# Squares of token tiles 8 to 11 moved from TensorE and VectorE to ScalarE, with a new order on every engine

## The chip, the cores and the metric

The kernel runs on one core of a Trainium2 chip. The metric is the device time of one execution in microseconds. A lower time is better.

## The reference

One transformer layer on 2048 tokens of width 640 in bfloat16: a LayerNorm, a linear attention with 32 heads of 20 numbers each (softmax feature maps of both signs), a projection with a residual, a second LayerNorm, and a gated bilinear feed-forward of width 1536 with a residual.

```python
def _A_ref(x, wqkv, w_phi, wo):
    qkv = (x @ wqkv).reshape(B, S, 3, H, Dh)            # -> q, k, v per head
    pq = jnp.einsum("bhsd,hdf->bhsf", q, w_phi)
    pk = jnp.einsum("bhsd,hdf->bhsf", k, w_phi)
    phi_q = concat([softmax(pq), softmax(-pq)], axis=-1)
    phi_k = concat([softmax(pk), softmax(-pk)], axis=-1)
    kv = jnp.einsum("bhsf,bhsd->bhfd", phi_k, v)
    z  = jnp.einsum("bhsf->bhf", phi_k)
    num = jnp.einsum("bhqf,bhfd->bhqd", phi_q, kv)
    den = jnp.einsum("bhqf,bhf->bhq", phi_q, z)[..., None] + 1e-6
    return (num / den).reshape(B, S, D) @ wo

h  = x + _A_ref(layernorm(x), wqkv, w_phi, wo)
h2 = h + ((g := layernorm(h) @ w_gate) * (layernorm(h) @ w_up)) @ w_down
```

The first `layernorm(x)` is what the change touches: for each token it needs the mean and the mean of the squares over 640 numbers.

## The kernel before, in words

The 2048 tokens are 16 tiles of 128. Each operation is recorded with `g.op` under the name of a unit (`U`). `ORDER` gives for each engine a written list of unit names; an engine carries out its operations in exactly that order, each one once what it needs is there. `Prog.place` walks through the five lists with the costs given to each operation (`t`, `lat`, `size`) and decides from them which of the rotating buffers an operation gets; it moves nothing. `Prog.finish` puts the semaphore waits between the engines. SP's list is a queue of DMA issues: loads, and transposes done by the DMA engines.

The names of the units: `wk` and `x0` to `x4` build the folded key weights, `t0` to `t4`, `wm`, `wq0` to `wq4` and `y0` to `y4` the folded query weights, `wv` and `c0` to `c4` centre the value weights. `lT4` to `lT15` are the transposed loads of a token tile (`xT`), `lx0` to `lx3` the plain loads of four token tiles each (`x_all`, so `lx2` holds tiles 8 to 11), `lwq`, `lwo`, `lg`, `lu`, `ld` the loads of the query, output, gate, up and down weights. `s0`, `s2`, `s4`, `s8`, `s12` are the statistics of token tiles 0-1, 2-3, 4-7, 8-11, 12-15. `k`, `v`, `q` with a tile number are the projections of keys, values and queries; `K` and `Q` normalise keys and queries. `A0` to `A14` accumulate keys times values, `Aout` brings that to SBUF, `n` is the numerator with its division, `h` the output projection with residual and second LayerNorm, `wo0` to `wo4` sum Wo's rows on ScalarE, `f` are feed-forward steps, `d` and `D` the down projection, and `G`, `H`, `S`, `T` sums for matrix products that need fewer multiplications.

All matrix products land in four PSUM buffers of two banks each (`p_ps`). A group of matmuls takes a buffer when one is free and gives it back when its last reader is through. For keys and queries (`softexp`) that is VectorE's maximum (L925), a product on VectorE (L928) and two exponentials on ScalarE (L933); for values one evacuation by ScalarE (L956).

The statistics are in `stats`. In the form for all tiles but 12 to 15, TensorE multiplies each of the five 128x128 blocks of a tile by itself and by a column of constants, 129 columns in all; the diagonal of the sum holds the sums of squares, which VectorE reads out with one multiply-and-sum pass over 128x128 per tile (L702), and the last column is the sum. For tiles in a group named in `ST_ACT`, TensorE only multiplies by the column of constants (one column), and ScalarE squares the tile in its natural layout (`x_all`, loaded by `lx`) and sums it on the way (`act_sum`, L650). GpSimd then makes the reciprocal standard deviation (`rs`, `nrs`) from both, and the exponentials of keys and queries and the evacuation of values need it.

Of the kernel before, what the change touches and what calls it, by code (L numbers as in the profile page):

```python
# [11 lines left out]
P = 128  # L12
S = 2048
D = 640
NT = S // P
NC = D // P
# [41 lines left out]
ST_ACT = (12,)  # L58
# [39 lines left out]
    "DVE":  # L98
# [16 lines left out]
    "ACT":  # L115
# [318 lines left out]
def _build(ctx, nc, A_x, A_wqkv, A_w_phi, A_wo, B_w_gate, B_w_up, B_w_down, out):  # L434
    g = Prog(nc, ctx)
# [8 lines left out]
    x_all = sb([P, NT, D], BF16, "x_all")  # L444
# [1055 lines left out]
```

## Time and profile before

| what | value |
|---|---|
| median of 3 runs | 267.67 us (267.41 to 268.5) |
| profiled execution | 267.55 us, span 265.8 us |
| granted clock | 0.999 |
| TensorE busy | 260.4 us (98% of the span) |
| TensorE weight loads busy | 200.0 us (75%) |
| VectorE busy | 222.7 us (84%) |
| ScalarE busy | 177.2 us (67%) |
| GpSimd busy | 190.1 us (72%) |
| data moved by DMA | 28.65 MB, mean 108 GB/s |

The span runs from the first to the last instruction of the profiled execution; the time also holds what lies around it. A matmul's end is modelled and matmuls overlap, so two matmul groups are compared by their starts, and a wait of TensorE is looked for on its weight loads (PEld), which come ahead of the matmuls. A row of the timeline has the start and the duration in us, the engine, the line, the operation, what it writes and reads, and in brackets the idle time ahead of it with what ended it. A row of the waits has who waited for whom, the total in us, how often, and the longest.

### The profile page before, as it was taken

To read this page: it belongs to the slowest core of one execution; us is meant where nothing else is said; L and a number is where in the kernel's file an instruction comes from. 1 tells how busy PE (TensorE), PEld (TensorE's weight loads), DVE (VectorE), ACT (ScalarE), POOL (GpSimd) and SP (SyncE) were. 2 spreads that over 40 slices of the span, in tenths; PEclk is the share of its full clock that TensorE was granted. 3 is DMA by queue.
4 is the path that set the end of the run, shared out by engine and by line. 5 is a ranking of instruction groups with operands and counts; after the bars stand their busy time and mean duration, and the time that the engine had idled before them with its cause. 6 is when DMAs were issued, how large, how long until landed. Compare 5 with 4: busy or idle time off the path is not lost.

```text
span 265.8 us, 6243 instructions
## 1 busy us (share of the span) xinstructions
PE 260.4 (98%) x2418; PEld 200.0 (75%) x2433; DVE 222.7 (84%) x417; ACT 177.2 (67%) x387; POOL 190.1 (72%) x243
## 2 busy tenths in 40 slices
PE   8999999999999999999999999999999999999995
PEld 8877777776877787777767887777777777777773
DVE  1999999999999876998999778988778788675683
ACT  2567999999857998769553695764857555645220
POOL 5446989999932889999974789359866575648652
PEclk9999999999999999999999999999999999999999
DMA  7997999903155789666856515300410401001012
GB/s 188 302 138 175 165 233 401 382 32 75 39 82 100 89 247 210 130 106 133 131 115 128 47 25 79 99 4 0 56 45 19 83 0 52 1 2 51 14 65 71
DMA packets 67390, 28.65 MB, mean 108 GB/s; under 512 B 57632, under 2 KB 66080, under 8 KB 67360
## 3 DMA queue, kind: packets, MB, share of 16 engines
q1 hardware_dynamic: 66432, 27.90, 48.7%
q10 hardware_dynamic: 928, 0.35, 0.5%
q8 instruction: 19, 0.31, 0.5%
q14 instruction: 11, 0.09, 0.1%
HBM read 11.82 MB, written 2.62 MB: 54 GB/s over the span
## 4 chain that ended last, share of the span: by engine, by line
PE 85%; DVE 5%; DMA 3%; ACT 3%; issue 1%; POOL 1%; SPq 0%; ACTq 0%
PE ps L657 60%; PE ps L1210 24%; DMA phiqT<-eq 3%; ACT eq L933 1%; DVE ob L1075 1%; PE ps L746 1%; DVE x_all L1093 1%; DVE ps L925 1%; DVE Sq L987 1%; ACT phiqT L1335 0%; POOL eq L999 0%; DVE rden L1073 0%; DVE phiqT L806 0%; ACT junk L650 0%; ACT eq L1220 0%
## 5 line engine op out<-in xcount | busy, mean ns | idle before, releaser
L657 PE MATMUL ps<-Wp,xT 128*128 128x320 bf16 (+1 forms) x606 | 89.1, 299 | 0.0
L657 PEld LDWEIGHTS ps<-Wp,xT 128*128 128x128 bf16 x606 | 58.0, 98 | 22.5 <-ACT phik L933 0.3
L1240 POOL TENSOR_TENSOR phik<-phik,gate 128x512 bf16<-128x512 bf16 x34 | 40.1, 1184 | 25.9 <-DVE phik L1237 25.5
L1220 ACT ACTIVATE eq<-ps 128x256 f32<-128x256 f32 x110 | 37.4, 386 | 23.0 <-PE ps L1210 18.6
L1210 PE MATMUL ps<-phik,Wgu 128*128 128x256 bf16 (+1 forms) x214 | 46.6, 299 | 0.2
L950 POOL TENSOR_TENSOR phik<-phik,Rk 128x1280 bf16<-128x1280 bf16 x16 | 37.4, 2357 | 5.8 <-DVE Rk L949 4.8
L657 PE MATMUL ps<-phik,Wgu 128*128 128x256 bf16 (+1 forms) x259 | 33.2, 280 | 0.1
L657 PEld LDWEIGHTS ps<-phik,Wgu 128*128 128x128 bf16 x260 | 25.0, 98 | 5.5
L1337 POOL TENSOR_TENSOR phiqT<-phiqT,x_all 128x320 f32<-128x320 f32 x26 | 21.7, 844 | 9.7 <-ACT phiqT L1335 9.6
L925 DVE TENSOR_REDUCE ps<-ps 128x1 f32<-128x640 f32 (+1 forms) x32 | 26.1, 818 | 2.8 <-PE ps L657 2.8
L1210 PEld LDWEIGHTS ps<-phik,Wgu 128*128 128x128 bf16 x228 | 21.9, 98 | 5.7 <-ACT eq L1220 0.2
L657 PE MATMUL ps<-vaug,phik 128*128 128x63 bf16 (+1 forms) x308 | 25.9, 238 | 0.0
L987 DVE TENSOR_REDUCE Sq<-eq 128x66 f32<-128x1320 bf16 x16 | 24.2, 1513 | 1.4 <-ACT eq L933 1.4
L1237 DVE TENSOR_TENSOR phik<-ps,eq 128x512 bf16<-128x512 f32 x28 | 19.1, 687 | 6.3 <-PE ps L1210 6.2
L1335 ACT ACTIVATE phiqT<-ps 128x320 f32<-128x320 f32 x26 | 11.4, 437 | 19.3 <-PE ps L657 19.2
L947 DVE TENSOR_REDUCE Ssum<-phik 128x64 f32<-128x1280 bf16 x16 | 23.3, 1460 | 0.0
L1235 DVE TENSOR_TENSOR gate<-ps,eq 128x512 bf16<-128x512 f32 x27 | 18.5, 685 | 5.2 <-PE ps L1210 2.9
L657 PEld LDWEIGHTS ps<-vaug,phik 128*128 128x128 bf16 x308 | 18.1, 97 | 5.3
L999 POOL TENSOR_TENSOR eq<-eq,rq 128x660 bf16<-128x660 bf16 x16 | 20.9, 1305 | 0.8
L933 ACT ACTIVATE eq<-ps,nb,rs 128x300 bf16<-128x300 f32 (+2 forms) x26 | 17.2, 689 | 6.1 <-DVE nb L928 4.5
L1342 DVE TENSOR_TENSOR outb<-ps,phiqT 128x320 bf16<-128x320 f32 x28 | 13.4, 487 | 6.9 <-PE ps L657 5.5
L1139 ACT ACTIVATE gate<-ps 128x256 bf16<-128x256 f32 (+1 forms) x26 | 10.4, 406 | 10.3 <-PE ps L657 9.6
(168 smaller groups left out, 526.2 us busy)
## 6 DMA issues: line engine op xcount, KB each, us to landing
x_all<-in_A_x_dram SPq DMA_DIRECT2D x4, 640.0 KB, 10.7
out_dram<-outb SPq DMA_DIRECT2D x14, 160.0 KB, 1.9
Wgu<-in_B_w_gate_dram SPq DMA_DIRECT2D x1, 1920.0 KB, 10.6
Wgu<-in_B_w_up_dram SPq DMA_DIRECT2D x1, 1920.0 KB, 16.3
vaug<-in_B_w_down_dram SPq DMA_DIRECT2D x1, 1920.0 KB, 8.5
Wp<-in_A_wqkv_dram SPq DMA_DIRECT2D x1, 800.0 KB, 5.0
phiqT<-in_A_wqkv_dram SPq DMA_DIRECT2D x1, 800.0 KB, 6.4
Wo<-in_A_wo_dram SPq DMA_DIRECT2D x1, 800.0 KB, 6.0
```

Of the source, the lines that this page charges most:

```text
L657: ins = e.matmul(o_, lhsT=l_, rhs=r_, start=s_, stop=p_, skip_group_check=True)
L925: g.op("DVE", lambda e: e.tensor_reduce(out=mx(), in_=src(), axis=AX.XY if len(src().shape) == 3 else AX.X, op=ALU.max, apply_absolute_val ...
L933: g.op("ACT", lambda e, s=s, sc=sc, to=to, of=of: e.activation(out=to(s), in_=of(), func=ACT.Exp, bias=nb[:, i:i + 1], scale=sc[:, t:t + 1 ...
L947: g.op("DVE", lambda e: e.tensor_reduce(out=Ssum[:, vs.i, :], in_=x, axis=AX.X, op=ALU.add), rd=R_phik[t], wr=vs.R, use=[vs], t=1.39, lat=1.5)
L950: g.op("POOL", lambda e: e.tensor_tensor(out=x, in0=x, in1=Rk[:, vr.i, :].unsqueeze(2).to_broadcast([P, 2 * H, DH]), op=ALU.mult), rd=vr.R ...
L987: g.op("DVE", lambda e: e.tensor_reduce(out=Sq[:, vs.i, :].rearrange("p (w g) -> p w g", w=NQ), in_=feat(0, NQ).rearrange("p w (g f) -> p ...
L999: return e.tensor_tensor(out=x, in0=x, in1=rq[:, vr.i, :].rearrange("p (w h) -> p w h", h=HW).unsqueeze(3).to_broadcast([P, NQ, HW, DH]), ...
L1210: ins = e.matmul(o_, lhsT=l_[0](c), rhs=m_, start=fr, stop=False, skip_group_check=True)
L1220: g.op("ACT", lambda e: e.activation(out=half(s[i], 256 * h, 256 * (h + 1)), in_=PS[v.i][:, bk, 256:512], func=ACT.Copy), rd=[v.R[bk]], wr ...
L1237: g.op("DVE", lambda e: e.tensor_tensor(out=hhT[:, hb_, ft, :], in0=PS[v.i][:, 1, :], in1=half(s[1]), op=ALU.add), rd=[v.R[1]] + s[1].R, w ...
L1240: g.op(eng, lambda e: e.tensor_tensor(out=hhT[:, hb_, ft, :], in0=hhT[:, hb_, ft, :], in1=gate[:, vg.i, :], op=ALU.mult), rd=R_out + vg.R, ...
L1337: g.op("POOL", lambda e: e.tensor_tensor(out=slot(x), in0=slot(x), in1=x_all[:, t, c], op=ALU.add), rd=x.R + [R_h[t]], wr=x.R, use=[x], t= ...
```

## The change

`ST_ACT` gets the group of tiles 8 to 11: their squares are summed by ScalarE on the natural tokens, and TensorE's 20 matmuls for them have one column in place of 129. VectorE's four read-outs of these tiles go. Several of the costs that `place` uses are set anew. The lists of all engines are written anew; ScalarE's list still begins with its first three entries (`in in in`). Shown are the heads of four lists and the changed lines of SP's.

```diff
@@ -55,7 +55,7 @@
...
-ST_ACT = (12,)
+ST_ACT = (8, 12)
...
@@ -73,77 +73,77 @@
     "PE":
-        "warm wk wk wk wk wk wk wk wk wk s0 wk x1 s0 x1 x3 wv wv x2 x0 x0 s2 x4 s2 k0 k0 k0 k0 k0 k3 k1 wm k2 v2 v3 s4 s4 s4 s4 "
-        "v5 k7 v7 k4 k6 v4 k5 y3 v0 y1 s8 s8 s8 s8 y4 k10 y2 y0 v1 s12 s12 k11 q0 s12 s12 k8 k9 v11 q1 v9 v6 k12 k13 v14 v10 v13 "
-        "k14 k15 q2 v8 v15 q5 q3 A0 A0 A2 A4 A6 A8 A2 A4 v12 A6 A8 A10 A10 A12 A14 A12 A14 n0 n1 n0 n1 q7 n0 q4 n1 h0 h1 n2 q6 h1 "
...
+        "warm wk wk wk wk wk wk wk wk wk wk x1 s0 s0 x1 x2 x3 wv wv x0 x0 x4 s2 s2 k0 k0 k0 k0 k0 k1 k3 wm v3 v2 k2 s4 s4 s4 s4 "
+        "k7 v7 k4 v5 k6 y3 v4 k5 y1 v0 s8 s8 s8 s8 k10 y4 y0 v1 y2 k11 s12 s12 s12 s12 q0 k9 k8 v11 q1 v9 k12 v6 k14 k13 v14 v13 "
+        "v10 k15 q2 v8 v15 v12 A0 A2 q3 A0 A4 A6 A8 q5 A2 A10 A4 A6 A8 A12 A10 A14 A12 A14 n0 n1 n0 n1 q7 n0 q4 n1 h0 h1 n2 q6 h1 "
...
     "DVE":
-        "wk in in wk in wk wk wk s0 s0 x1 x3 s0 c2 c1 c0 s2 s2 c4 s2 k0 k0 c3 k3 k3 k1 k1 K0 k2 wq2 wq4 K0 K1 k2 s4 s4 s4 s4 s4 "
-        "K3 K1 k7 wq0 K3 k7 K2 k4 k4 k6 K2 k6 K7 k5 y3 k5 K7 y1 K4 s8 s8 s8 s8 s8 K4 k10 K5 k10 K6 k11 K6 k11 q0 K5 q0 s12 K10 k8 "
-        "k9 k8 K11 K10 K11 q1 k9 K8 q1 Q0 k12 K8 k13 k12 K9 k13 Q0 Q1 K9 K12 k14 Q1 k14 k15 K12 K13 k15 q2 K13 K14 q2 K14 K15 q3 "
...
+        "wk in in in wk wk wk wk s0 s0 s0 x1 x3 c3 c2 s2 c4 s2 s2 k0 k0 c1 c0 k1 k1 k3 wq2 K0 k3 wq4 K0 K1 k2 k2 s4 s4 K1 s4 s4 "
+        "s4 k7 K3 wq0 k7 k4 K3 k4 K2 k6 y3 k6 K2 K7 y1 K7 k5 k5 s8 K4 K4 k10 K5 k10 K6 k11 K6 s12 K5 k11 q0 q0 K10 k9 k8 k8 K11 "
+        "q1 K10 k9 K11 K8 q1 k12 Q0 k12 K9 K8 k13 k14 k13 Q0 K9 k14 K12 Q1 K12 Q1 k15 K13 k15 K13 K14 q2 K14 q2 K15 q3 K15 q3 Q2 "
...
     "ACT":
-        "in in in wk wk wk x2 x0 x4 k0 k0 k3 wm k1 k1 v2 v3 k3 k2 wq1 k2 v5 wq3 k7 v7 k7 k4 k4 v4 k6 k6 k5 v0 k5 s12 y4 y2 s12 y0 "
-        "v1 k10 k10 s12 k11 k11 q0 q0 s12 v11 k8 k8 v9 k9 k9 v6 q1 q1 wo0 v14 k12 k12 v10 k13 wo1 k13 v13 k14 k14 wo2 v8 k15 k15 "
-        "v15 q2 wo4 q2 wo1 q3 q3 v12 wo3 q5 wo3 q5 wo2 wo0 n0 wo4 n1 q7 q7 q4 q4 q4 q4 h0 h1 f0.4.0 h0 f0.4.0 f0.10.0 f0.10.0 "
-        "f0.0.0 q6 f0.0.0 q6 q6 q6 h2 f0.1.0 h3 f0.1.0 q8 f0.11.0 f0.11.0 q8 q8 q8 f0.8.0 f0.8.0 f0.7.0 f0.7.0 h1 f0.5.0 f0.5.0 "
...
+        "in in in wk wk wk x2 x0 x4 k0 k0 wm k1 v3 k1 v2 k3 k3 s8 k2 k2 wq3 s8 wq1 v7 k7 v5 k7 k4 k4 s8 v4 k6 k6 s8 v0 k5 k5 y4 "
+        "y0 s12 v1 y2 k10 s12 k10 s12 k11 k11 q0 q0 s12 v11 k8 k8 v9 k9 k9 q1 v6 q1 k12 k12 wo1 v14 wo0 v13 k13 k13 v10 k14 wo1 "
+        "k14 wo2 v8 k15 k15 v15 v12 wo3 wo2 q2 q2 q3 q3 wo4 wo3 wo4 q5 q5 wo0 n0 n1 q7 q7 q4 q4 q4 q4 h0 h1 f0.10.0 f0.10.0 "
+        "f0.4.0 f0.4.0 h0 f0.0.0 f0.0.0 q6 q6 q6 h2 q6 f0.1.0 f0.1.0 h3 f0.11.0 q8 f0.11.0 f0.7.0 q8 q8 f0.8.0 q8 f0.8.0 f0.7.0 "
...
     "POOL":
-        "in in in in in in in in in in in in pad in in wk s0 s0 s0 in in s0 s2 s0 s2 s2 s0 s2 s2 s2 K0 s4 s4 s4 s4 s4 s4 K3 K1 K2 "
-        "K7 s8 s8 s8 s0 s8 s8 in s8 K4 K6 K5 s12 in s12 s12 s12 s12 K11 pad s12 K10 K8 Q0 Q0 K9 Q1 Q1 K12 K13 K14 K15 Q2 Q2 Q3 Q3 "
-        "Q5 s4 s2 Q5 Q7 Q7 f0.4.0 f0.10.0 s8 Q4 Q4 f0.0.0 h2 f0.1.0 h2 f0.11.0 Q6 h3 Q6 f0.8.0 h3 f0.7.0 f0.5.0 s12 Q8 f0.6.0 Q8 "
-        "T0 h0 f0.2.0 f0.3.0 T0 h1 h0 f0.9.0 Q10 Q10 T2 Q9 T2 h1 h7 Q14 h5 Q14 h7 h7 Q9 h5 h5 T0 T1 Q11 h4 T1 Q11 h6 h4 Q12 h6 "
...
+        "in in in in in in in in in in in pad in in in wk s0 s0 in s0 s0 s0 in s2 in in s2 s0 s2 s2 s2 s2 K0 s4 s4 s4 s4 s4 s4 K1 "
+        "K3 K2 K7 s8 s8 s8 s8 s8 s8 s0 K4 K5 s2 K6 pad s12 s12 s8 s12 s12 K10 s12 s12 K11 K8 Q0 K9 Q0 Q1 K12 K13 Q1 K14 K15 Q2 Q2 "
+        "Q3 Q3 Q5 Q5 Q7 Q7 f0.4.0 s4 f0.10.0 Q4 Q4 h2 h2 f0.0.0 f0.1.0 Q6 f0.11.0 s12 Q6 f0.8.0 h3 f0.7.0 h3 f0.5.0 Q8 f0.6.0 Q8 "
+        "f0.2.0 T0 T0 f0.9.0 Q10 h1 f0.3.0 T2 Q10 h0 h1 h0 T2 Q14 h7 Q14 h7 h5 h7 h5 Q9 Q9 h5 T1 T0 Q11 Q11 T1 h6 h6 h4 h6 h4 "
...
     "SP":
-        "in in in in in in in lwq t4 lT7 lT4 t2 lT5 lT6 t3 t1 t0 lx3 lT10 lT15 lT9 lT11 lT8 lT13 lT14 lT12 lx0 lwo lg lu lx2 lx1 "
-        "Q0 Q1 Q0 Q1 Q2 Q2 Q3 Q3 Q5 Q5 n2 n3 Q7 Q7 Q4 ld Q4 Q6 n7 n5 Q6 Q8 Q8 h3 n4 h2 Q10 Q10 n6 Q14 Q14 Q9 n8 Q9 h5 h7 Q11 Q11 "
-        "n10 h4 h6 n9 Q12 Q12 n11 Q15 n14 Q13 Q13 Q15 n12 h8 n15 h11 n13 h9 h10 d0 d1 D0.1 h14 D0.1 h12 h13 h15 D1.0 D1.0 D1.1 "
+        "in in in in in in in lwq t2 lT4 lT5 t4 lT6 lT7 lx2 t3 t0 t1 lT15 lT8 lwo lT9 lT11 lT10 lT13 lx3 lT14 lT12 lg lx0 lu Q0 "
+        "Q0 lx1 Q1 Q1 Q2 Q2 Q3 Q3 Q5 n2 Q5 n3 Q7 Q7 ld Q4 n7 Q6 Q4 Q6 n5 h3 Q8 Q8 h2 n4 Q10 Q10 n6 Q14 Q14 Q9 h5 Q9 h7 n8 Q11 Q11 "
+        "n10 h4 h6 n9 Q12 Q12 n11 Q15 n14 Q13 Q15 Q13 n12 d1 d0 n15 h8 n13 h11 h10 h9 h14 D0.1 h15 D0.1 D1.0 D1.0 h13 h12 D1.1 "
...
@@ -546,9 +546,9 @@
-        return g.op(eng, lambda e: e.dma_start(out_, in_), wr=wr, dma=("w", 8), t=0.5, lat=0.4 if at else 1.9, size=mb / 0.38, at=at)
-
-    def transpose(out_, in_, rd, wr, use=(), t=1.27, size=1.07, lat=0.5, at=0.0):
+        return g.op(eng, lambda e: e.dma_start(out_, in_), wr=wr, dma=("w", 8), t=0.5, lat=0.4 if at else 0.6, size=mb / 0.38, at=at)
+
+    def transpose(out_, in_, rd, wr, use=(), t=1.27, size=0.45, lat=0.3, at=0.0):
@@ -585,10 +585,10 @@
-        transpose(lambda: xT[:, t, :, 0:P], lambda: A_x[0, P * t:P * (t + 1), :], [], [R_xT[t]], t=1.5, size=0.75, lat=1.25 if at else 2.75, at=at)
+        transpose(lambda: xT[:, t, :, 0:P], lambda: A_x[0, P * t:P * (t + 1), :], [], [R_xT[t]], t=1.5 if at else 1.4, size=0.75 if at else 0.62, lat=1.25 if at else 2.1, at=at)
-        load(x_all[:, 4 * b:4 * b + 4, :], A_x[0, 4 * P * b:4 * P * (b + 1), :].rearrange("(t p) n -> p t n", p=P), [R_x[b]], 1.2)
+        load(x_all[:, 4 * b:4 * b + 4, :], A_x[0, 4 * P * b:4 * P * (b + 1), :].rearrange("(t p) n -> p t n", p=P), [R_x[b]], 0.9)
@@ -684,7 +684,7 @@
-            g.op("PE", f, rd=[R_xT[t], R_one, R_xone], wr=[v.R[j // 2]], use=[v], t=0.125 if act else 0.282, lat=0.275 if act else 0.43)
+            g.op("PE", f, rd=[R_xT[t], R_one, R_xone], wr=[v.R[j // 2]], use=[v], t=0.19 if act else 0.282, lat=0.34 if act else 0.43)
@@ -816,7 +816,7 @@
-        g.op("PE", lambda e: mms(e, mean_mms(PS[v.i][:, 0, :], range(NC), 0)), rd=R_Wnat + [R_one], wr=v.R, use=[v], t=0.64, lat=0.79)
+        g.op("PE", lambda e: mms(e, mean_mms(PS[v.i][:, 0, :], range(NC), 0)), rd=R_Wnat + [R_one], wr=v.R, use=[v], t=0.73, lat=0.88)
@@ -1001,7 +1001,7 @@
-                      b.R + [R_pad], [R_phiqT[bb][k][tt]], [b], t=0.254 * (w1 - w0), size=0.214 * (w1 - w0)))
+                      b.R + [R_pad], [R_phiqT[bb][k][tt]], [b], t=1.3, size=0.5, lat=0.35))
@@ -1369,7 +1369,7 @@
-        transpose(lambda: WT[:, 0, a, :], lambda: A_wqkv[:, P * a:P * (a + 1)], [], [R_WT[0][a]], t=1.5, size=0.75, lat=2.75)
+        transpose(lambda: WT[:, 0, a, :], lambda: A_wqkv[:, P * a:P * (a + 1)], [], [R_WT[0][a]], t=1.4, size=0.62, lat=2.1)
@@ -1383,7 +1383,7 @@
-    load(Wo[:, :, 0:D], A_wo.rearrange("(c p) n -> p c n", p=P), R_Wo, 1.5)
+    load(Wo[:, :, 0:D], A_wo.rearrange("(c p) n -> p c n", p=P), R_Wo, 0.95)

```

98 rows, old and new, of the table ORDER are left out of this document.

## The prediction

> **What bounds the kernel now.** I read the head of the page, then busy time by stage, then what each engine waited for, then single rows of the timeline.
>
> ```profile
> span 265.8 us, 6243 instructions
> PE 260.4 (98%) x2418; PEld 200.0 (75%) x2433; DVE 222.7 (84%) x417; ACT 177.2 (67%) x387; POOL 190.1 (72%) x243
> PE 85%; DVE 5%; DMA 3%; ACT 3%; issue 1%; POOL 1%; SPq 0%; ACTq 0%
> ```
>
> TensorE is on 85% of the chain that ended last and is busy 98% of the span. The average hides the stage that the change touches. Busy time by stage (stretch, its length, then PE, PEld, DVE, ACT, POOL, the granted clock, the DMA share and GB/s):
>
> ```profile
> 20.00:70.00 50.00, 49.94 (x490) 37.23 (x488) 49.57 (x94) 46.95 (x72) 45.58 (x41) 1.00 0.71 199
> 70.00:80.00 10.00, 9.71 (x167) 7.81 (x164) 9.26 (x23) 5.88 (x13) 5.58 (x7) 1.00 0.40 60
> ```
>
> From 20 to 70 us four engines run at 91% or more: TensorE 49.94, VectorE 49.57, ScalarE 46.95, GpSimd 45.58 of 50. ScalarE has 3.05 us left, VectorE 0.43. What TensorE lost to waits is seen on its weight loads. From 4.7 to 80 us, and then from 80 us on (total, times, longest):
>
> ```profile
> PEld ps L657 <- DVE sm L698: 0.6, 2, 0.4
> PEld ps L657 <- DVE Phi L1040: 0.4, 1, 0.4
> PEld ps L657 <- ACT phik L933: 0.3, 1, 0.3
> PEld ps L657 <- DMA phiqT<-in_A_wqkv_dram: 0.3, 1, 0.3
> PEld ps L657 <- DVE sxx L702: 0.2, 1, 0.2
> ```
>
> ```profile
> PEld ps L657 <- ACT eq L933: 0.9, 2, 0.5
> PEld ps L1210 <- ACT eq L1220: 0.8, 4, 0.2
> PEld ps L657 <- issue: 0.2, 1, 0.2
> PEld ps L1210 <- issue: 0.2, 1, 0.2
> ```
>
> That is 1.8 + 2.1 = 3.9 us in all. So no order of the same work can win more than 3.9 us, while a bad order can lose without such a limit. Shorter TensorE work shortens the kernel, but only if the other three full engines keep up.
>
> **The change part by part.**
>
> *TensorE.* For tiles 8 to 11, 20 matmuls with 129 columns become 20 with one column. The two kinds, each with the row that starts next:
>
> ```profile
> 34.13 1.30 PE L657 MATMUL ps<-xT 128*128 128x129 bf16 x20
> 35.26 0.48 PE L657 MATMUL ps<-Phi,phiqT 128*128 128x140 bf16 x6
> ...
> 42.38 0.39 PE L657 MATMUL ps<-ones,xT 128*128 128x1 bf16 x10
> 42.63 2.65 PE L657 MATMUL ps<-Wp,xT 128*128 128x320 bf16 x18
> ```
>
> From start to start the 20 wide ones hold TensorE 35.26 - 34.13 = 1.13 us; ten narrow ones (tiles 14 and 15 today) 42.63 - 42.38 = 0.25, so twenty 0.50. Saved: 0.63 us. The Trainium skill, "TensorE: Matmul & The Clock Gate", section "LDWEIGHTS (loading the stationary operand)", speaks against this: a load of 128 weight columns takes about 128/1.2 = 107 ns whatever is multiplied, and "Back-to-back issue gap" says that load and matmul together set the spacing; a narrow matmul with weights of its own would then save nothing, and the sum would be 0.63 us higher. The row just quoted has 25 ns per pair of load and matmul and decides for the saving.
>
> *VectorE and ScalarE.* VectorE loses four multiply-and-sum passes, ScalarE gains four squares over 128x640.
>
> ```profile
> 36.53 0.28 DVE L702 CUSTOM_DVE_ANT_0 t<-ps,ident 128x128 f32<-128x128 f32 x1
> ...
> 37.37 0.55 DVE L949 RECIPROCAL Rk<-Ssum 128x64 f32<-128x64 f32 x1
> ```
>
> ```profile
> 36.23 0.74 ACT L650 ACTIVATE junk<-x_all 128x640 bf16<-128x640 bf16 x1
> ...
> 36.95 1.30 ACT L861 ACTIVATE Wp<-ps 128x640 bf16<-128x640 f32 x2
> ```
>
> VectorE: 37.37 - 36.53 = 0.84 us less. ScalarE: 36.95 - 36.23 = 0.72 us for one square with its read-out, 2.88 us for four. Does that fit? ScalarE's waits from 15.4 to 66.4 us, then five of its rows: the first key exponential, the evacuations of values tiles 2 and 3, the exponential ahead of which the first new square stands in ScalarE's new order, and the evacuation of values tile 15:
>
> ```profile
> ACT phik L933 <- DVE nb L928: 2.7, 2, 2.2
> ACT vaug L956 <- PE ps L657: 1.6, 3, 0.6
> ACT phik L933 <- POOL nrs L716: 0.5, 1, 0.5
> ACT vaug L956 <- POOL rs L714: 0.4, 1, 0.4
> ```
>
> ```profile
> 15.50 0.88 ACT L933 ACTIVATE phik<-ps,nb,rs 128x640 bf16<-128x640 f32 x1 [2.19 <-DVE nb L928]
> ...
> 20.34 0.80 ACT L956 ACTIVATE vaug<-ps,rs 128x640 bf16<-128x640 f32 x1 [0.60 <-PE ps L657]
> 21.70 0.80 ACT L956 ACTIVATE vaug<-ps,rs 128x640 bf16<-128x640 f32 x1 [0.56 <-PE ps L657]
> ...
> 23.16 0.88 ACT L933 ACTIVATE phik<-ps,nb,rs 128x640 bf16<-128x640 f32 x1
> ...
> 65.69 0.80 ACT L956 ACTIVATE vaug<-ps,rs 128x640 bf16<-128x640 f32 x1
> ```
>
> Of the 5.2 us of waits, 2.2 lie before 15.50; 3.0 us are left. Into these go 2.88 us of squares and one short copy that the new order moves ahead (about 0.1): 2.98. So ScalarE reaches the end of values 15 no later than today only if it never waits again. But two of the waits, 0.60 and 0.56 us for TensorE, come before 23.16, so ahead of the first new square, and no square can fill them. The new order puts these two evacuations between other exponentials, which may close part of them: I take 0.7 to 1.2 us of lag. At nothing it would cost 0 (bound from below: all gaps filled), at worst the whole 2.88 (no gap filled).
>
> TensorE feels this lag through PSUM: four buffers, and key, value and query groups give one back only after ScalarE has read it.
>
> ```profile
> 64.92 0.88 ACT L933 ACTIVATE phik<-ps,nb,nrs 128x640 bf16<-128x640 f32 x1
> ```
>
> ```profile
> 65.74 1.84 PE L657 MATMUL ps<-Wp,xT 128*128 128x300 bf16 x12
> 67.42 2.69 PE L657 MATMUL ps<-vaug,phik 128*128 128x63 bf16 x86
> ```
>
> The second exponential of keys 15 ends at 65.80; the last ten of the 12 matmuls from 65.74, queries 3, need the latter's buffer and start just above 66.0 (67.42 less ten at 0.14). So TensorE is at most 0.2 us behind ScalarE here. In the new order the accumulation over keys and values takes that place after values 12, and waits for the same buffer: 65.80 + 0.7 to 1.2. From there to its end the new order has queries 3 and 5 inside where the old had queries 3 and values 12: within 0.1 us the same. So the stage ends about 0.5 us later (lower end of the lag), not 0.63 earlier: ScalarE eats 1.1 us.
>
> *GpSimd.* Two constant fills (0.7 us each) leave its row of key multiplications for its idle start, and the variances of tiles 8 to 11 wait for the fourth square, not VectorE. In the new order that square follows the exponentials of keys 6, some 3 us ahead of VectorE's 37.37. I cost both at nothing: 45.58 of 50 busy leaves cover; without it keys 4 to 6 behind them would slip.
>
> *SP's queue.* The load of tokens 8 to 11 moves from near the end of the queue to behind the sixth transpose that follows the query weights' load, ahead of three weight transposes, and Wo's load ahead of the transposes of tiles 9, 11 and 10; the load of tokens 12 to 15 falls back. Its new place in the queue is issued at 17.8 now, right after these transposes; the one load like it is this:
>
> ```profile
> 15.22 2.60 SPq L553 DMA_TRANSPOSE xT<-in_A_x_dram  x2
> ```
>
> ```profile
> x_all<-in_A_x_dram SPq DMA_DIRECT2D x1, 640.0 KB, 4.7
> ```
>
> 17.8 + 4.7 = 22.5, against ScalarE free for the square at 22.6 to 23.2: just in time, cost 0. The upper end is in the rivals. Wo's 800 KB can delay tiles 9 to 11 by up to 3 us; TensorE needs them about 2 us after today's landing. I take 0, with 1 us as the other end. The token load that now comes after the first query transposes is needed only past 80 us.
>
> *The rest of the order.* Behind 80 us the same instructions are shuffled. One move has a row: the down-weight load is issued ahead of both transposes of query tile 4, not between them.
>
> ```profile
> 93.47 0.58 SPq L549
> 94.10 8.54 DMA phiqT<-eq
> ```
>
> That transpose lands 8.5 us after its issue, behind 1920 KB, and the chain runs on to a TensorE wait of 0.5 us. Loaded earlier, I take 0.3 us off. All else I take as 0, between -1.8 (the remaining waits there go) and +2 (as many again).
>
> **Sum.** -0.63 + 1.1 - 0.3 = +0.2 us on the profiled execution, 267.55 us (span 265.8 plus 1.75 around it), 0.12 under the median of 267.67: 267.9 us. About 0.5%, 1.3 us, is what a measurement can tell from no change.
>
> **The rivals.**
>
> *The saving lands whole.* VectorE, with 0.43 us left in 50, may be what paces the stage; with 0.84 less there, keys and queries reach ScalarE earlier and its first gaps close. Then TensorE's 0.63 stands: 267.67 - 0.63 - 0.3 = 266.7. For it: VectorE has no wait to speak of. Against it: ScalarE's sum above. The Trainium skill's "Perfetto Trace Analysis", section "Optimizing Scalar/DVE Operations", takes this side: with a full VectorE, work may well be handed to ScalarE. It assumes room there, and the stage rows show 3.05 us.
>
> *Tokens 8 to 11 come late: slower.* Between 16 and 22.3 us the DMA engines stood still about 1 us in 40 slices of 0.16:
>
> ```profile
> DMA  9984235899822349899779994000000999979325
> ```
>
> If the load sits behind transposes held by such a stop it lands at 24 or later. ScalarE waits 1.0 to 1.5 us at its first square; behind it in ScalarE's order stand keys 2's exponentials and values 7, whose buffers TensorE needs. All later gaps being spent, it comes on top: 267.9 + 1.4 = 269.3. It decides from a landing of about 23.5 us.
>
> *The new order is better all along.* More than half of the 3.9 us of waits goes: 267.67 - 0.63 - 1.2 = 265.8. For it: the waits at 75 and 105 us follow from order. Against it: all else was already hidden.
>
> **How the numbers follow.** ScalarE takes the saving back, 0.42: 267.9. Whole saving 0.22: 266.7. Late tokens 0.26: 269.3, mostly past +1.3. Better all along 0.10: 265.8. Faster: 0.10 and a little of the second, 0.13. Slower: 0.29, 0.22 from late tokens and the rest from a lag near its upper end. Within 0.5%: 0.58. The range leaves out the best case and the tail of late tokens: 266.4 to 269.7; the likeliest case alone spans 267.3 to 268.7.
>
> **What would show it.** Right: 20 one-column matmuls for tiles 8 to 11 in 0.50 us; ScalarE above 49 of 50 us between 20 and 70; new TensorE waits for ScalarE in that stage, about 1 us; values 15 read about 0.7 us later than 65.69; the transpose of query tile 4 landing earlier. Late tokens would show as a ScalarE wait on the token load before its first square. Wrong: ScalarE below 49 with TensorE ending the stage 0.6 us earlier, or a wait that no step here names, after 80 us above all.

## The result, and the profile after

The changed kernel takes 270.07 us in the median of 12 executions (268.24 to 271.3), the kernel before 267.63 beside it: ratio 1.0076, 95% interval 1.0054 to 1.0098. A second series of the same kernel (e5 below) gave 269.21 (268.22 to 269.87, ratio 1.0058, 1.0038 to 1.0078). So the change costs 1.8 to 2.4 us by the medians (1.6 to 2.0 by the ratios), more than the 0.5% named as the bound. The forecast 267.9 was too low: the median 270.07 lies 0.4 above the upper end of its range, and the ratio, 1.0076 of 267.67, puts the time at that end (269.7). The executions spread over 3 us where those of the kernel before spread over 1.3. They fall into two groups, five from 268.24 to 268.63 and seven from 269.73 to 271.3: part of the cost comes and goes. The profiled execution took 270.41, span 268.7.

Head of its page, then busy time between 20 and 70 us (stretch, its length, PE, PEld, DVE, ACT, POOL, clock, DMA share, GB/s):

```profile
span 268.7 us, 6261 instructions
PE 262.1 (98%) x2433; PEld 199.1 (74%) x2433; DVE 224.3 (83%) x409; ACT 179.8 (67%) x395; POOL 190.6 (71%) x243
PE 59%; ACT 15%; SPq 6%; DVE 6%; DMA 5%; POOL 5%; issue 2%; ACTq 0%; DVEq 0%
```

```profile
20.00:70.00 50.00, 49.42 (x461) 35.33 (x460) 48.47 (x85) 49.61 (x82) 43.73 (x41) 1.00 0.80 192
```

ScalarE has gone from 46.95 to 49.61 of 50, VectorE from 49.57 to 48.47, TensorE from 49.94 to 49.42: ScalarE now has 0.39 us left there. Busy shares over the whole span hardly move (TensorE 98% in both); it is the chain that shows the change, where TensorE fell from 85% to 59% and ScalarE rose from 3% to 15%.

What TensorE's weight loads waited for, over the whole span (total us, times, longest):

```profile
PEld ps L657 <- issue: 2.2, 6, 0.8
PEld ps L657 <- ACT phik L933: 1.8, 5, 0.5
PEld ps L657 <- ACT eq L933: 1.8, 2, 1.5
PEld ps L1210 <- ACT eq L1220: 0.7, 3, 0.3
PEld ps L657 <- ACT vaug L956: 0.7, 3, 0.3
PEld ps L657 <- DMA Wp<-in_A_wqkv_dram: 0.6, 1, 0.6
```

Two of these rows carry most of the result (the first has no cause that the profile shows; it was 1.0 us before). The key exponentials (`phik`) made TensorE wait 0.3 us in all before, 1.8 now, in five pieces inside the stage. The query exponentials (`eq`) have one wait of 1.5 us, at 106 us, where nothing of the squares is left. The chain of waits there, in order of time (start, us, what):

```profile
98.97 0.67 POOL phik L1145
99.64 0.08 issue
99.72 0.20 POOL vpe L1111
99.93 0.57 SPq L553
100.50 0.04 issue
100.54 4.39 DMA phiqT<-eq
104.93 0.02 issue
104.95 0.04 ACTq L401
104.99 0.05 issue
105.04 0.10 ACT eq L933
```

This is the second transpose of query tile 4. Before, it was issued at 94.10 and landed at 102.64. Now it stands in SP's list behind `n7` and behind the first transpose of `Q6`. `n7` waits 2.0 us for VectorE's numerator and is issued at 97.47; the first transpose of `Q6` follows at 98.85, right behind GpSimd's product for it (97.52 to 98.82), and its issue takes 1.65. So Q4's second transpose is issued at 100.54 and lands at 104.93, and ScalarE and TensorE stand behind it.

All the time can be put in one sum. I add up TensorE's late starts: from one matmul's start to the next, what goes beyond the first one's own streaming time (columns times 0.42 ns, at least 25 ns), where that is over 25 ns. Span less late starts is then the bare work of TensorE and what lies ahead of it.

```
                      span    late starts by stretch of the span (us)      span less
                              4.7-12   12-78   78-136   136-end   sum       late starts
before               265.80    1.16    1.18    0.79     0.17     3.30      262.50
after                268.68    1.33    2.59    2.23     0.64     6.79      261.89
e5  after again      267.37    1.27    3.10    0.70     0.73     5.80      261.57
e1  Q4 together      267.21    0.87    3.21    0.69     0.61     5.38      261.83
e2  no squares       267.26    1.95    2.10    0.68     0.07     4.80      262.46
e3  new head         266.08    0.87    2.71    0.44     0.19     4.21      261.87
e4  new tail         265.85    1.10    1.18    0.72     0.38     3.38      262.47
e6  less on ScalarE  266.77    0.99    2.84    0.65     0.45     4.93      261.84
e7  Wo's load back   265.88    0.93    2.41    0.56     0.11     4.01      261.87
e8  squares alone    267.96    1.08    4.13    0.65     0.22     6.08      261.88
e9  no square work   265.12    0.75    1.94    0.47     0.11     3.27      261.85
e10 both in SP       266.71    0.76    2.74    1.17     0.16     4.83      261.88
e11 Q4 late          270.80    2.33    1.23    4.29     0.37     8.22      262.58
e12 down load back   266.27    1.15    1.23    1.06     0.27     3.71      262.56
```

The last column has two values: about 262.5 for kernels with the 20 wide matmuls, about 261.87 for those with narrow ones. The difference, 0.63 us, is the saving that the prediction gave to TensorE. By itself the column does not show it, since the streaming times that are counted differ by nearly that much already; the rows do. Where no wait falls into them, the 20 narrow matmuls for tiles 8 to 11 take 0.50 us from start to start and the 20 wide ones 1.13, in every kernel. What decides is the sum ahead of it: 3.30 before, 6.79 after. (e5 alone reads 261.57; one late start too many may have been counted there.)

### The profile page after: what moved, and what is told of

Read it like the earlier page. It is cut to its first block, busy times and chain, and to the rows that moved or that the text cites. A ratio compares the mean times of both kernels' runs of the same rounds, so it can differ in the third digit from the quotient of the medians.

```text
span 268.7 us, 6261 instructions
## 1 busy us (share of the span) xinstructions
PE 262.1 (98%) x2433; PEld 199.1 (74%) x2433; DVE 224.3 (83%) x409; ACT 179.8 (67%) x395; POOL 190.6 (71%) x243
## 4 chain that ended last, share of the span: by engine, by line
PE 59%; ACT 15%; SPq 6%; DVE 6%; DMA 5%; POOL 5%; issue 2%; ACTq 0%; DVEq 0%
PE ps L657 34%; PE ps L1210 25%; SPq L553 6%; ACT phik L933 5%; ACT eq L933 4%; DMA phiqT<-eq 3%; ACT junk L650 3%; DVE Sq L987 2%; DMA x_all<-in_A_x_dram 2%; POOL Wp L1261 2%; ACT vaug L956 2%; POOL eq L999 1%; DVE ps L925 1%; ACT gate L1139 1%; SPq L549 1%
## 5 line engine op out<-in xcount | busy, mean ns | idle before, releaser
L657 PEld LDWEIGHTS ps<-Wp,xT 128*128 128x128 bf16 x606 | 57.4, 98 | 24.2 <-ACT phik L933 1.8
L1210 PE MATMUL ps<-phik,Wgu 128*128 128x256 bf16 (+1 forms) x228 | 50.5, 304 | 0.0
L657 PE MATMUL ps<-phik,Wgu 128*128 128x256 bf16 (+1 forms) x260 | 33.7, 281 | 0.0
L1237 DVE TENSOR_TENSOR phik<-ps,eq 128x512 bf16<-128x512 f32 x27 | 18.4, 687 | 6.1 <-PE ps L1210 5.8
```

Of the source, the lines that this page charges most:

```text
L657: ins = e.matmul(o_, lhsT=l_, rhs=r_, start=s_, stop=p_, skip_group_check=True)
L1210: ins = e.matmul(o_, lhsT=l_[0](c), rhs=m_, start=fr, stop=False, skip_group_check=True)
```

## The experiments

The theory from this profile: ScalarE is full in the stage and TensorE pays for it there (about 1 us), and the rest is in SP's queue, whose new order leaves landings without slack. The first rival: neither, it is the new order of the engines as a whole. The verdicts below compare each kernel with the kernel before on the same chip, 267.43, 267.43 and 267.44 in the three batches.

**e1: Q4's two transposes together again.**

```diff
 SP:
-... ld Q4 n7 Q6 Q4 Q6 n5 h3 ...
+... ld Q4 Q4 n7 Q6 Q6 n5 h3 ...
```

> The changed kernel with one edit on SP's queue: behind the down-weight load, both transposes of query tile 4 come first and the numerator 7 transpose and both transposes of query tile 6 after them (Q4 Q4 n7 Q6 Q6 in place of Q4 n7 Q6 Q4 Q6). Theory A (queue order): the second transpose of query tile 4 stood behind two transposes that were not ready, was issued at 100.5 us and released ScalarE's exponential at 105.0, and TensorE waited 1.35 us at 106.1. With the edit that wait falls under 0.5 us and the median falls by about 1 us, to about 269.0. Rival (the 1920 KB load itself holds it up): the wait stays above 1 us and the time within 0.4 us of 270.07.

Measured: 268.24 (267.46 to 269.85), ratio 1.0038 (1.0018 to 1.0057), against 270.07 and 269.21 of the changed kernel. The wait at 106 us is gone: late starts between 78 and 136 us fall from 2.23 to 0.69. But the profile shows another one, inside the stage:

```profile
PEld ps L657 <- DMA xT<-in_A_x_dram: 1.2, 1, 1.2
PEld ps L657 <- ACT phik L933: 1.2, 3, 0.5
```

That is at 34.9 us, for a transpose of the tiles behind Wo's load, which took 7.45 us to land; the DMA engines stood still twice in that time (the last section has these stops). So Q4's place does cost time: 1.0 to 1.8 us by the medians. By the ratios it is 0.5 to 1.0, and e5's interval (1.0038 to 1.0078) overlaps with this one, so the size is loose. A second landing can be late as well.

**e2: the new order without the squares.**

```diff
-ST_ACT = (8, 12)
+ST_ACT = (12,)
 DVE: one s8 -> five;  ACT: the four s8 taken out; all else as changed
```

> The new order on every engine, but the squares of tiles 8 to 11 go back to TensorE and VectorE (their four entries leave ScalarE's list, four come back into VectorE's). Theory B (ScalarE's queue): TensorE's waits of 2.0 us between 12 and 70 us come from ScalarE's 2.88 us of squares; without them they fall below 0.8 us, TensorE's work rises by 0.63, the key-value accumulation ends at about 74.4 us in place of 74.9, and the median falls by 0.5 to 0.8 us, to about 269.4. Rival (the order itself): the waits stay near 2 us, and the median rises by 0.6 to about 270.7.

Measured: 269.27 (268.67 to 269.63), ratio 1.0064 (1.0051 to 1.0077). With 20 wide matmuls and ScalarE's squares gone, the new order still costs. In the profile 1.2 us of it is a wait for the value weights at 9.35 us, 0.8 more late starts up to 12 us than before; in the stage 2.10 stand against 1.18. So the order without the squares has about 0.9 us more late starts in the stage, and the squares make no clear difference to the total in this order. But 0.86 us of it is one wait, up to 44.4 us, and the chain that leads to it runs through the four read-outs, put back on VectorE into an order written without them. The wait can come from them as well as from the order. The rival is half right.

**e3: new lists up to the end of the KV accumulation, old ones behind; e4: the other way round.**

```diff
 each list of ORDER:
+e3: the changed list up to the last A14 / Aout / q5 / Q3, then what is left, in the old order
+e4: the old list up to there, then what is left, in the changed order
```

> Up to the end of the key-value accumulation the lists of the changed kernel, squares included; from there the lists of the kernel before, for what is left. If the loss before 75 us is about 1.0 us (theory B) and the rest lies after 80 us (theory A and other order), the median is 1.0 to 1.3 us above the kernel before, about 268.8, and the TensorE wait near 105 us is about 0.4 us. Rival (everything follows from the late stage end): above 269.7. Rival (the head is harmless): within 0.4 us of before.

> The mirror image: up to the end of the key-value accumulation the lists of the kernel before, without the squares on ScalarE; from there the lists of the changed kernel. Theory A plus other waits after 80 us: the median is 1.5 to 2.0 us above the kernel before, about 269.4, with a TensorE wait above 1 us near 105 us. Rival (the tail is harmless by itself and only suffers from the late head): within 0.5 us of before.

Measured: e3 268.11 (267.5 to 269.04), ratio 1.0023 (1.0006 to 1.0039); e4 267.98 (267.58 to 270.02), ratio 1.003 (1.0014 to 1.0047). The parts add to 1.0053, near e5's 1.0058 and below the first series. Both came in below the theory's 268.8 and 269.4. e3's late starts beyond those of the kernel before are all in the stage (2.71 against 1.18). e4's profile has 0.08 us more than the kernel before in all, and Q4's second transpose, issued at 99.05, landed 2.8 us later with no wait; yet two of its twelve executions took 269.29 and 270.02. So the wait near 105 us that the theory asked for is not in this profile, and what the new tail costs varies by execution.

**e5: the changed kernel again.**

> The changed kernel unchanged, for a second profile of it. Theory of the landings (its times fall in two groups because some DMA landings that it reads without slack are late in some executions): the median again 268.2 to 270.5, and if this profile is of a short execution, Q4's second transpose of phi(q) has taken under 3.5 us and the 1.35-us wait of TensorE at 106 us is under 0.5. Rival (the wait at 106 us is in the order itself): the wait is there in this profile too, whatever the time.

Measured: 269.21 (268.22 to 269.87). The profiled execution (269.1) has no wait at 106 us: Q4's second transpose was issued at 100.25, 0.29 us earlier than in the first profile, and landed 2.82 us later (103.07), not 4.39. A stop of the DMA engines falls at another time. The first profile from 88 to 110 us, then e5's from 88 to 106, each in 40 slices; 0 is less than a tenth busy:

```profile
DMA  9393956955889999999999299993906937739129
```

```profile
DMA  9479389099494899999999999948999958900589
```

In the first profile a stop that begins at 103.7 holds packets for some 0.9 us, while the transpose is under way. In e5 the stop begins at 103.4, 0.3 us after it has landed. e5 has late starts of 0.60 at 28.0 and 0.65 at 149.5 instead. So the 1.35 us is not in every execution, as the theory said; but this execution was not a short one, and it is not one wait that makes the spread.

**e6: centring of query weights 1 and 3 from ScalarE to VectorE (in e3).**

```diff
-            if a in (1, 3):
+            if a in ():
 ACT: wq1, wq3 taken out;  DVE: wq3 and wq1 behind K3 wq0 and K3
```

> The new lists to the end of the KV accumulation and the old ones behind it (268.11 as it was run before), with the centring of query weights 1 and 3 moved from ScalarE (0.73 us each) to VectorE (0.30 each). Theory of ScalarE's lag (ScalarE has no room between 20 and 70 us, so its PSUM buffers come back late): with 1.46 us off ScalarE the last value matmul ends 0.5 to 0.6 earlier, TensorE's waits for ScalarE between 12 and 70 us fall from about 1.5 to under 0.8 us, and the time is 267.4 to 267.7. Rival (the new order of TensorE and of the queue costs it, not ScalarE's load): the time stays at 268.1.

Measured: 268.17 (267.62 to 268.65), ratio 1.0025 (1.0016 to 1.0035): nothing. A miss for the theory as it stood. From 12 to 75 us, e3 and then e6:

```profile
12.00:75.00 63.00, 62.16 (x679) 45.59 (x677) 61.08 (x108) 56.93 (x94) 51.93 (x53) 1.00 0.73 177
```

```profile
12.00:75.00 63.00, 61.95 (x673) 45.61 (x671) 62.11 (x111) 56.10 (x92) 52.08 (x53) 1.00 0.72 178
```

VectorE's 1.03 us more took it to 62.11 of 63, and ScalarE's new room was spent waiting for VectorE:

```profile
36.40 0.89 ACT L933 ACTIVATE phik<-ps,nb,rs 128x640 bf16<-128x640 f32 x1 [0.65 <-DVE nb L928]
```

TensorE then waited 1.04 us at 37.0 for that exponential. The price on VectorE was too low, though: one of the two centrings took 1.22 us there (from 28.29), where the other four such operations of this profile took 0.38, and no run here shows why. So e6 does not show what the move is worth at its planned price.

**e7: Wo's load back behind tile 12's transpose (in e3).**

```diff
 SP:
-... lT8 lwo lT9 lT11 lT10 lT13 lx3 lT14 lT12 lg ...
+... lT8 lT9 lT11 lT10 lT13 lx3 lT14 lT12 lwo lg ...
```

> The same mixed lists (new to the end of the KV accumulation, old behind it), with the load of Wo moved back behind the transpose of tile 12 in SP's queue. Theory of the landings: the transposes of tiles 9 to 11 land some 2 us earlier, the runs lie closer together (under 268.5 in nine of ten), and the median is 267.7 to 268.0. Rival (the order of that queue does not matter): median and spread as before, 268.1 and 267.5 to 269.0.

Measured: 268.24 (267.35 to 268.74), ratio 1.0022 (1.001 to 1.0034). Neither the median nor the spread clearly differs from e3's. The late landing at 35 us that e1's profile shows is possible, but Wo's place is not what makes e3 0.7 us slower than the kernel before.

**e8: the squares alone, in the old order.**

```diff
-ST_ACT = (12,)
+ST_ACT = (8, 12)
 ACT: ... wq3 k7 v7 k7 [s8] k4 k4 [s8] v4 k6 [s8] k6 [s8] k5 v0 ...
 DVE: five s8 -> one
 SP:  ... t0 lx2 lT10 lT15 lT9 lT11 lT8 lx3 lT13 lT14 lT12 ...
```

> The squares of tiles 8 to 11 on ScalarE alone, in the old order of every list (only the four squares put into ScalarE's list, the load of the natural tokens of tiles 8 to 11 ahead of the transposes of tiles 10, 15, 9, 11 and 8, and the 20 wide summing matmuls made narrow). Theory of ScalarE's lag: TensorE saves 0.63 us and gets it back as waits for ScalarE, 2.6 us of squares against some 1.5 us of idle time there: 267.7 to 268.4. Rival (the saving lands whole): 266.8. Rival (only the new order costs): 266.8 to 267.4.

Measured: 270.2 (269.65 to 271.13), ratio 1.0108 (1.0087 to 1.0128), more than even the theory said. Three of its six executions, 270.58 to 271.13, have a mean granted clock of 0.994; the three at 1.00, the profiled one among them, took 269.65 to 269.81, some 2.3 us above the kernel before. Up to 78 us:

```profile
PEld ps L657 <- DVE sm L698: 1.6, 3, 1.1
PEld ps L657 <- ACT vaug L956: 1.0, 1, 1.0
PEld ps L657 <- issue: 0.7, 1, 0.7
PEld ps L657 <- ACT Wp L861: 0.6, 2, 0.3
```

I had put the four squares into 10 us in which ScalarE had only 0.5 us of idle time; from 29.55 us on its rows follow each other without a gap. Late starts in the stage grew from 1.18 to 4.13. The saving of 0.63 is there (261.88) and is lost almost five times over. So the new order is not a fault beside the squares: it spreads them out, and it avoids most of the cost that they have in this place.

**e9: narrow matmuls without the squares' work (in e3).**

```diff
-                act_sum(x_all[:, t, :], ACT.Square, sxx[:, t:t + 1], [R_x[t // 4]], [R_sxx[t]])
+                if i0 != 8: ...the same...
+                elif j == 3: one activation over 128x4 writes all four sums
```

> The new lists to the end of the KV accumulation, the old ones behind it (268.11 and, on a second kernel like it, 268.24), with the narrow summing matmuls but without the four squares: one activation over 128x4 stands for them, so the variances of tiles 8 to 11 are wrong numbers. That takes some 2.6 us off ScalarE and puts nothing on another engine. Theory of ScalarE's lag: TensorE's waits between 12 and 78 us fall from 2.71 to about 1.6 or less, the last matmul of the KV accumulation ends 1.0 to 1.2 earlier than 74.45, and the time is 266.9 to 267.1. Rival (the new order of the other engines sets it, and ScalarE has room enough): the time stays at 267.9 to 268.2 and the waits at 2.4 to 2.7.

Measured: 267.02 (266.79 to 268.37), ratio 0.9991 (0.9978 to 1.0004), 1.09 below e3: as the theory of ScalarE's lag had it. The numerator behind the KV accumulation starts at 74.76 in e3 and at 73.85 here:

```profile
74.76 0.49 PE L657 MATMUL ps<-Phi,phiqT 128*128 128x63 bf16 x10
```

```profile
73.85 0.49 PE L657 MATMUL ps<-Phi,phiqT 128*128 128x63 bf16 x10
```

The late starts in the stage fell less than expected, from 2.71 to 1.94 and not to 1.6; before has 1.18. So of the 1.5 us that e3 has too much there, about half goes with the squares' work and half stays, in a stage where ScalarE has room again (48.07 of 50). That half is the order's.

**e10: both places in SP's queue put back, in the changed kernel.**

```diff
 SP: e1's edit and e7's
```

> The changed kernel with both suspected places of SP's queue put back: Wo's load behind the transpose of tile 12, and the two transposes of Q4 one behind the other. Theory of the landings: no wait of TensorE over 0.6 us for Q4 at 106 us and none over 0.6 for tiles 8 to 11 at 35 us, median 267.8 to 268.3, against 269.2 to 270.1 of the changed kernel. Rival (the changed kernel's other new order is what costs): 269 or more.

Measured: 268.79 (268.44 to 269.37), ratio 1.005 (1.0036 to 1.0064). Neither of the two big waits is in the profile, and the six executions lie within 0.9 us (e5's six within 1.65, the first twelve within 3). But the median missed: the stage still has 2.74 us of late starts, and between 78 and 136 us there are 1.17 in pieces of 0.44 at most. Taking the landings away may narrow the time; it does not bring it back.

**e11: Q4's second transpose late, in the kernel before.**

```diff
 SP:
-... Q4 ld Q4 Q6 n7 n5 Q6 ...
+... Q4 ld n7 Q6 Q4 n5 Q6 ...
```

> The kernel before, with one move alone: Q4's second transpose stands behind n7 and Q6's first in SP's queue, as in the changed kernel. Theory of the landings: it is issued 4 to 6 us later, TensorE's wait at 105 us grows from 0.38 to between 1.0 and 3.0 us, and the time is 267.9 to 269.5, with a wider spread than before's. Rival (the wait at 106 us belongs to a pause of the DMA engines that would have come anyway): within 0.3 us of the kernel before.

The edit is not quite one move alone: `n7` also comes ahead of Q6's first transpose.

Measured: 271.73 (271.12 to 272.52), ratio 1.0152 (1.0135 to 1.0169), beyond the upper end of what was expected. From 78 to 140 us, and the end of the chain that leads there:

```profile
PEld ps L657 <- ACT eq L933: 2.9, 2, 2.5
```

```profile
99.60 0.52 POOL rs L1113
100.12 0.15 SPq L553
100.28 0.04 issue
100.32 5.56 DMA phiqT<-eq
105.88 0.02 issue
```

It is the chain of the changed kernel again: `n7` waits for VectorE, query tile 6's first transpose is issued at 99.00, right behind GpSimd's product for it (97.67 to 98.98), then Q4's at 100.32, landing at 105.88. Late starts from 78 to 136 us grow by 3.5 us, from 0.79 to 4.29. Only 2.40 of the 4.29 is the wait itself, which ends at 108.49. Right behind it the granted clock is 0.5 from 108.6 to 112.0 us, which adds 1.6. It is the 7 in the page's row (40 slices of 6.8 us):

```profile
PEclk9999999999999999799999999999999999999999
```

All five executions of e11 have a mean granted clock of 0.994. Another 1.17 of this execution lies ahead of 12 us, in a wait for the value weights that this edit doesn't touch. So this small move costs over 3 us where the list around it was not made for it, some 2.0 by the longer wait and 1.6 by the clock behind it.

**e12: the down-weight load behind Q4's second transpose, in the kernel before.**

```diff
 SP:
-... Q4 ld Q4 Q6 ...
+... Q4 Q4 ld Q6 ...
```

> The kernel before, with the load of the down weights one place further back, behind Q4's second transpose. The step of the prediction that gave 0.3 us for this place: the transpose lands at about 97.5 instead of 102.6, TensorE's wait of 0.38 us at 104.8 goes, and the time is 267.05 to 267.2. Rival (what frees one wait is taken by the next, Q6's or the load's own): within 0.1 us of the kernel before.

Measured: 268.33 (267.9 to 271.17), ratio 1.0046 (1.0024 to 1.0068): slower, beside both expectations. The transpose did land at 96.25 instead of 102.64 and TensorE's 0.38 us at 104.8 went. But the load, issued 1.3 us later, landed 1.7 us later (103.65 against 101.96) and pushed back what stands behind it: query tile 6's first transpose landed at 104.22 instead of 103.22. New late starts at 106.6 and 109.6 us follow, and those between 78 and 136 us add up to 1.06, not 0.79. That is 0.27 of the 0.47 us by which the profiled execution's span is longer (268.01). Two executions at 270.23 and 271.17 are not explained; the second has a granted clock of 0.994, the first 1.00.

No kernel tried beats the one before; e9, which leaves work out, only equals it.

## Why the prediction was right, and where it was wrong

*TensorE's saving: right.* Twenty one-column matmuls, start to start 35.89 - 35.39 = 0.50 us:

```profile
35.39 0.64 PE L657 MATMUL ps<-ones,xT 128*128 128x1 bf16 x20
35.89 1.38 PE L657 MATMUL ps<-Wp,xT 128*128 128x320 bf16 x9
```

This settles how the rule of the Trainium skill that was weighed bears on this case ("TensorE: Matmul & The Clock Gate", "LDWEIGHTS (loading the stationary operand)": a load of 128 columns takes about 107 ns). One behind the other, twenty loads would take some 2.1 us, an estimate from that figure. One load's row does last 96 ns here, but the loads overlap, and the twenty pairs take 0.50.

*ScalarE: right in mechanism, close in size.* ScalarE reads values 15 at 66.69, 1.0 us later, inside the 0.7 to 1.2:

```profile
66.69 1.49 ACT L956 ACTIVATE vaug<-ps,rs 128x640 bf16<-128x640 f32 x2
```

TensorE's waits for `phik` grew by 1.5 us. The squares' work is worth 1.09 us (e3 less e9), which is the 1.1 that was put down for it. What the step left out is the other half of the stage's late starts: the new order costs there some 0.8 us by itself (e9; e2 is no clean test of it). So the stage ends about 1.0 us later, not 0.5: the numerator behind it starts at 75.22, not 74.09, and 0.17 of that lies ahead of 12 us.

*The tokens of tiles 8 to 11: nearly right.* The load landed 0.8 us later than the 22.5 estimated, and the first square starts with it, at 23.30, with ScalarE waiting about 0.26 us:

```profile
22.26 0.90 ACT L933 ACTIVATE phik<-ps,nb,nrs 128x640 bf16<-128x640 f32 x1
23.30 0.74 ACT L650 ACTIVATE junk<-x_all 128x640 bf16<-128x640 bf16 x1
```

Issued at 17.91, landed at 23.28, short of the 23.5 from which the rival decides. That rival's number, 269.3, was near the result by luck: its mechanism was not what happened.

*GpSimd at nothing: right*, no wait for it in the stage in this profile. *Wo's load at nothing: right in the median* (e7), with a wait of 1.2 us in one execution of e1.

*The failed step: the rest of the order, -0.3 us.* It looked at one of the two moves in that place. With the load ahead of both transposes of query tile 4, the second does land earlier when the two stand together (101.55 in e1, 102.64 before), but the first now stands behind the 1920 KB too: in the changed kernel it landed at 101.41 instead of 94.81. The second move put Q4's second transpose behind `n7` and `Q6`, and on an in-order queue an issue inherits every wait of those ahead of it. It was issued 6.4 us later and landed later, not earlier, at 104.93 in the first profile and 103.07 in e5's; and where a stop of the DMA engines met it TensorE waited 1.35 us. The new tail alone (e4) came out 0.55 us slower by the median, 0.8 by the ratio, where -0.3 was forecast. Putting Q4's transposes together gains 1.0 to 1.8 us by the medians in e1, but only 0.4 to 1.3 in e10, where Wo's load was moved as well. Moving the load the other way (e12) frees the wait and pays it again, so the gain was not to be had in that way either. "All else" was taken as 0 between -1.8 and +2: from 78 us on the late starts grew by 1.9 us in the first profile and by 0.5 in e5's.

*The saving lands whole* fell: VectorE did get 1.1 us of room, and its waits don't pace the stage. The Trainium skill's advice that went with it ("Perfetto Trace Analysis", "Optimizing Scalar/DVE Operations", hand work from a full VectorE to ScalarE) holds here only with room on ScalarE; e8 shows the price without it, 2.3 us at full clock, and in e6 handing other work back to VectorE gained nothing either.

What stays open: why executions of one kernel differ by up to 3 us, and what the new tail costs beside Q4's place. The last section has what the traces show of it; e7 and e10 show that neither of the two places in the queue is the whole cause.

## What to carry to other kernels

Before an operation is moved to another engine, add up that engine's idle time in the stage after the point where the operation may run, not its busy share over the kernel: 2.88 us of work against 3.05 us of idle time, part of it too early to be used, cost 1.1 us. When an in-order queue is reordered, follow every issue that changed place to what now stands ahead of it, and ask whether one of those waits for another engine; the waits it inherits can cost more than the bytes. And split a change that reorders everything into head and tail, and into order and work, before explaining its time.

## What the runs showed of the hardware

*All 16 DMA engines stop together.* In every trace they do nothing for 0.9 to 1.6 us, three to seven times in the first 130 us. The busy share of the engines in 40 slices, the kernel before from 86 to 92 us, then the changed one from 34 to 40 us, where there is one stop of over 2 us:

```profile
DMA  9999200000899992000000659999900004000045
```

```profile
DMA  4947799999999999999000000000000000999999
```

In the first row the zeros are also times without work. In the second, a load of 640 KB and two transposes were under way when the engines stopped. The packets that were on their way then show a duration of 0.9 to 3.0 us, 10 to 28 of them at once. The stops lie at 12.6, 19.4, 90.0 and 103.5 us in the profile of before, at 13.3, 36.1, 99.3 and 103.7 in that of after, at 10.1, 18.6, 78.3 and 103.4 in e5: some recur near 13 and 104 us, others move. What causes them no run here shows. Whether a stop reaches TensorE depends on what is under way: the one near 103.5 met Q4's second transpose in the first profile, where TensorE then waited 1.35 us; in e5 the transpose had just landed, and TensorE did not wait for it. That fits a spread of 3 us for the changed kernel, but the other executions have no trace to show it.

*A DMA transpose's issue is not free.* On SP's queue most take 1.2 to 1.3 us and some more, up to 3.9 in the changed kernel, and they land 2.5 to 8.6 us after their issue. The kernel before's longest, 8.54, is the one behind the 1920 KB of the down weights.

*TensorE's clock can fall behind a long wait.* In e11 TensorE stood still for 2.4 us and then had half its clock for 3.4 us: a matmul of 340 columns took 0.285 us from start to start, 0.84 ns a column, against 0.42 elsewhere. Behind the wait of 1.35 us in the changed kernel's profile the clock stayed at 1.00. A mean clock of 0.994 also stands at three of e8's six executions and one of e12's; every other execution has 0.998 or more. What sets it off no run here shows.
